# One transposition per block in the later attention chunks: GpSimd adds the two squares of exponentials, VectorE splits them again with triangular masks

## The chip, the cores and the metric

The kernel runs on one core of a Trainium2 chip. The metric is the device time of one execution in microseconds (us). Engines are named as in the profile: PE is TensorE (matrix products), PEld its weight loads, DVE is VectorE, ACT is ScalarE, POOL is GpSimd, SP the engine that issues most DMAs.

## The reference

Attention with 4 sink keys and a window of 128 keys over 4 batches, 8 heads, 768 positions and head size 64, then a two-layer feed-forward on the 3072 tokens that come out (512 to 2048 to 512, with a squared relu between).

```python
scores = (q @ k.T) / sqrt(64)
keep = (key < n_sink) | ((query - key >= 0) & (query - key < window))
a = exp(where(keep, scores, -1e9) - max);  a = a / (sum(a) + 1e-9)
x = (a @ v).transpose(0, 2, 1, 3).reshape(3072, 512)
r = maximum(x @ w_in, 0);  out = (s * r * r + b) @ w_out
```

## The kernel before, in words

**Chunks.** The 3072 tokens are cut into 8 chunks of 384 (half a batch, three blocks of 128 queries). Attention of a chunk gives its x, and the first layer (`l1_steps`, line 680: 16 steps of 12 products `h`) reads x. The attention of the later chunks is woven into the first layer of the chunks ahead of them. Chunks 0 and 2 have code of their own (`first_slots`, `second_slots`); the other six go through `attn_slots`, and only these six are changed. The second layer (`second_layer`, line 805) follows when all chunks are through.

**A unit** is one head and one block of 128 queries; there are 6 x 8 x 3 = 144. Because the window is 128 keys, a block of queries sees two squares of 128 x 128 scores: the *own* square (keys of the same block, where only key <= query is kept) and the square *before* (keys of the block before, where only key > query is kept), and 8 sink columns. The first block of a sequence has no square before; this is so for 16 of the 144 units.

- `unit_a` (slot t): two products into a PSUM bank `sc` (lines 349, 350), DVE adds the mask into SBUF tile `sm` and takes the maximum (354), ACT takes the exponential in place with its sum (360), POOL copies the sink columns into `psk` (362).
- `unit_b` (slot t + 3, `LB`): PE transposes the square before and the own square into a bank `tp` (373, 374), and ACT copies both to the head's tile `tt` (377). After the last block of an odd head come four small DVE operations on the sums and a POOL copy (382 to 387).
- `unit_c` (slot t + 5, `LC`, last block of an odd head): PE multiplies V by the `tt` of both heads into `o` (399), ACT copies `o` to `xm` (403); for every second pair also `ts` and `xsk` (407 to 410).
- `unit_d` (slots t + 7 and t + 8, every second pair): two products `os` and `zb` (421, 423), two DVE operations (424, 425), an ACT cast (426) and a POOL subtraction (427) write x.
- `prep_head`, two slots ahead of a head: ACT and DVE split q and k into parts (330 to 335).

`sm` has SMB = 5 buffers, `tt` has TTB = 4, and PSUM banks rotate among eight.

**Order.** The main loop sorts all pieces by a due position among the first layer's steps and emits them; one attention slot falls to 7 or 8 products `h`, and the steps that prepare the second layer's weights (`early_w2`) are spread in between. A scheduler then fixes the order on each engine; each engine works in that order, and waits where data or a buffer isn't ready. Apart from a few pinned instructions, order is not written by hand.

Of the kernel before, what the change touches and what calls it, by code (L numbers as in the profile page):

```python
# [8 lines left out]
F32 = mybir.dt.float32  # L9
# [5 lines left out]
ALU = mybir.AluOpType  # L15
AX = mybir.AxisListType

P = 128
B, H, S, D = 4, 8, 768, 64
NS = 8  # L20
BLK = 3
CH = BLK * P
# [6 lines left out]
BIG = 3e38  # L29
MDT = mybir.dt.bfloat16  # L30
WUP = 256.0
SMB, TTB = 5, 4
WARM0 = 14
VB = 4
POOLED = 2
# [11 lines left out]
def tile_kernel(ctx, tc, qT, kT, k0, v, vsk, n_sink, window, w1, w2, s, b, out):  # L47
    nc = tc.nc
# [6 lines left out]
    def ps(name):  # L55
        return pools[0].tile([P, 512], F32, tag="a", name=name)
# [5 lines left out]
    wk = wk_cm.__enter__()  # L62
# [18 lines left out]
    ident = identr.bitcast(F32)  # L81
# [5 lines left out]
    msk = wk.tile([P, 3 * W + P + NS], MDT, tag="msk", name="msk", bufs=1)  # L87
    m_1, m_odd, m_even = (msk[:, j * W:(j + 1) * W] for j in range(3))
    m_0 = msk[:, 3 * W:]

# [22 lines left out]
    rel, rel1, low, upp, kix, snk, tmp, tm2 = (sc0[:, j, :] for j in range(8))  # L115


    def mask(out, keep):
        return nc.vector.tensor_scalar(out=out, in0=keep, scalar1=BIG, scalar2=-BIG, op0=ALU.mult, op1=ALU.add)
# [36 lines left out]
    def constants3():  # L156
        pin = tc.keep_in_program_order

        for i, sel in enumerate(sels):
            spread = wk.tile([P, P], F32, tag="y", name="spread", bufs=1)  # L160
            pin(nc.gpsimd.memset(spread, 0.0))
            for j in (i, 2 + i):
                nc.gpsimd.affine_select(
                    out=spread[96:P].rearrange("p (a d) -> p a d", a=2),
                    in_=spread[96:P].rearrange("p (a d) -> p a d", a=2),
                    pattern=[[1, 2], [0, D]], compare_op=ALU.not_equal, fill=1.0, base=2 * j, channel_multiplier=-1)
            nc.scalar.copy(sel, spread)
        for t in psks:
            pin(nc.gpsimd.memset(t, 0.0))
        pin(nc.vector.tensor_tensor(out=tmp[:, :NS], in0=low[:, :NS], in1=snk[:, :NS], op=ALU.mult))  # L170
        nc.vector.tensor_tensor(out=tmp[:, :NS], in0=snk[:, :NS], in1=tmp[:, :NS], op=ALU.subtract)
        pin(nc.vector.scalar_tensor_tensor(out=tm2[:, :NS], in0=rel1[:, :NS], scalar=w_ap, in1=snk[:, :NS],
                                           op0=ALU.is_ge, op1=ALU.mult))
        mask(m_0[:, :NS], tmp[:, :NS])
        mask(m_1[:, 2 * P:], tm2[:, :NS])
        pin(mask(m_even[:, P:P + NS], snk[:, :NS]))
        cp = lambda **a: pin(nc.gpsimd.tensor_copy(**a))
        upm, lom = m_full[2][:, P:2 * P], m_full[2][:, 2 * P:]
        cp(out=m_0[:, NS:], in_=lom)
        for m, l0 in ((m_1, P), (m_even, P + NS), (m_odd, P)):  # L180
            cp(out=m[:, :P], in_=upm)
            cp(out=m[:, l0:l0 + P], in_=lom)
        cp(out=m_odd[:, 2 * P:], in_=m_even[:, P:P + NS])
# [153 lines left out]
    def unit_a(k, h, i):  # L337

        hd = k.heads[h]
        pp = k.pairs[h // 2]  # L340
        g = k.half * BLK + i
        u = (k.c * H + h) * BLK + i
        if k.half == 0:
            c0, n = ((0, P + NS), (NS, W), (P + NS, W))[i]
        else:
            c0, n = ((0, W), (P, W), (W, W))[i]
        sc = ps("sc")
        qs = slice(i * P, (i + 1) * P)
        nc.tensor.matmul(sc[:, :n], hd.qs[:, qs], hd.kh[:, c0:c0 + n], start=True, stop=False)  # L349
        nc.tensor.matmul(sc[:, :n], hd.qs[:, qs], hd.kl[:, c0:c0 + n], start=False, stop=True)  # L350
        m = m_0 if g == 0 else m_1 if g == 1 else m_odd if g % 2 else m_even
        uu = slice(u, u + 1)
        sm = wk.tile([P, W], F32, name="sm", tag="sm", bufs=SMB)
        nc.vector.tensor_tensor_reduce(out=sm[:, :n], in0=sc[:, :n], in1=m, scale=-0.125, scalar=BIG,  # L354
                                       op0=ALU.add, op1=ALU.min, accum_out=negm[:, uu])

        k.cc[(h, i)] = (sm,) + ((NS, None, 0) if g == 0 else (P, 0, 2 * P) if g % 2 else (P + NS, 0, P))
        s0 = k.cc[(h, i)][3]
        hh = h % 2
        nc.scalar.activation(sm[:, :n], sm[:, :n], AF.Exp, bias=negm[:, uu], scale=-1.0, accum_out=pp.zz[:, i, hh:hh + 1])  # L360
        r0 = h % 4 * NS
        nc.gpsimd.tensor_copy(out=pp.psk[:, i, :96].rearrange("p (t x) -> p t x", t=3)[:, :, r0:r0 + NS],  # L362
                              in_=sm[:, s0:s0 + NS].unsqueeze(1).to_broadcast([P, 3, NS]))

    def unit_b(k, h, i):

        sm, c0, p0, _ = k.cc.pop((h, i))
        hd = k.heads[h]
        if i == 0:
            hd.tt = wk.tile([P, 8 * P], F32, name="tt", tag="tt", bufs=TTB)  # L370
        tp = ps("tp")
        if p0 is not None:
            nc.tensor.transpose(tp[:, :P], sm[:, p0:p0 + P], ident)  # L373
        nc.tensor.transpose(tp[:, P:2 * P], sm[:, c0:c0 + P], ident)  # L374

        a, z = (P if p0 is None else 0), 2 * P
        nc.scalar.copy(hd.tt[:, i * z + a:(i + 1) * z], tp[:, a:z])  # L377
        pp = k.pairs[h // 2]
        if h % 2 == 1 and i == BLK - 1:
            zr = wk.tile([P, 2, BLK, 2], F32, tag="zr", name="zr")  # L380
            zh = wk.tile([P, BLK, 2], F32R, tag="zh", name="zh")
            nc.vector.tensor_scalar(out=zr[:, 0], in0=pp.zz, scalar1=1e-9, scalar2=None, op0=ALU.add)
            nc.vector.reciprocal(out=zr[:, 1], in_=zr[:, 0])
            nc.vector.tensor_copy(zh, zr[:, 1])
            r0 = 96 + h // 2 % 2 * 2
            nc.gpsimd.tensor_copy(out=pp.psk[:, :, r0:r0 + 2], in_=zh.bitcast(F32))
            nc.vector.tensor_tensor(out=pp.psk[:, :, r0 + 4:r0 + 6], in0=zr[:, 1], in1=zh.bitcast(F32), op=ALU.subtract)
# [41 lines left out]
    def attn_slots(chunks):  # L429


        units, ahead = [], {}
        for k in chunks:
            for pr in range(H // 2):
                h, t0 = 2 * pr, len(units)
                units += [(k, h + hh, i) for hh in range(2) for i in range(BLK)]
                todo = ((-5, load_pair, pr), (-5, load_keys, h), (-2, load_sinks, pr), (-2, prep_head, h), (-2, load_keys, h + 1),
                        (1, prep_head, h + 1))
                for d, fn, a in todo:
                    ahead.setdefault(max(t0 + d, 0), []).append((fn, k, a))  # L440
        n = len(units)

        def slot(t):
            def f():
                for fn, k, a in ahead.get(t, ()):
                    fn(k, a)
                for fn, lag in ((unit_a, 0), (unit_b, LB), (unit_c, LC),
                                (lambda *u: unit_d(*u, -1), LC + LD), (lambda *u: unit_d(*u, 0), LC + LD + 1)):
                    if 0 <= t - lag < n:
                        fn(*units[t - lag])  # L450
            return f

        return [slot(t) for t in range(n + LC + LD + 1)]
# [571 lines left out]
    k, slots = first_slots()  # L1025
# [16 lines left out]
    t2 = H * BLK * t1 - LEAD  # L1042
    dt = (n_last - LEAD - t2) / len(rows)
    todo = [(max(t * t1 - LEAD, 0.3), f) for t, f in enumerate(plain)] + [(t2 - 2, constants3), (t2, scalars)]
    todo += [(t2 + t * dt, f) for t, f in enumerate(rows)]
    todo += [(NF + (t + 0.5) * (n_last - LEAD - NF) / n_early, lambda: next(early)()) for t in range(n_early)]
# [97 lines left out]
```

## Time and profile before

| | |
|---|---|
| median of 3 runs | 707.59 us (705.12 to 709.23) |
| the profiled execution | 706.58 us |
| its span from the first to the last instruction | 704.7 us |
| PE, PEld | busy 687.7 us (98%), 645.0 us (92%) |
| DVE, ACT | busy 506.0 us (72%), 505.1 us (72%) |
| POOL | busy 102.5 us (15%) |

The profile is of one execution; its time is 1.9 us more than its span. Busy shares are means over stages: start (to about 100 us), first layer with the later attention (100 to about 400 us), rest of the first layer (to about 450 us), second layer. Product records overlap, since products are pipelined, so the duration of one is more than what it adds to PE's time.

### The profile page before, as it was taken

To read this page: it belongs to the slowest core of one execution; us is meant where nothing else is said; L and a number is where in the kernel's file an instruction comes from. 1 tells how busy PE (TensorE), PEld (TensorE's weight loads), DVE (VectorE), ACT (ScalarE), POOL (GpSimd) and SP (SyncE) were. 2 spreads that over 40 slices of the span, in tenths; PEclk is the share of its full clock that TensorE was granted. 3 is DMA by queue.
4 is the path that set the end of the run, shared out by engine and by line. 5 is a ranking of instruction groups with operands and counts; after the bars stand their busy time and mean duration, and the time that the engine had idled before them with its cause. 6 is when DMAs were issued, how large, how long until landed. Compare 5 with 4: busy or idle time off the path is not lost.

```text
span 704.7 us, 13755 instructions
## 1 busy us (share of the span) xinstructions
PE 687.7 (98%) x4858; PEld 645.0 (92%) x4858; DVE 506.0 (72%) x1266; ACT 505.1 (72%) x1155; POOL 102.5 (15%) x249
## 2 busy tenths in 40 slices
PE   8999999999999999999999999999999999999994
PEld 4686789999999999999999999999999999999994
DVE  5999974765864765765766526688979897888883
ACT  3899778788788888888888636576666666657560
POOL 2303011322321331331331210000000000000000
PEclk9999999999999999999999999999999999999998
DMA  8952264466456566454453149933535344443522
GB/s 167 412 199 86 95 193 140 127 214 230 135 189 229 152 226 226 125 178 143 150 181 123 68 180 316 320 97 102 164 104 176 94 150 120 120 150 102 169 60 65
DMA packets 61182, 114.10 MB, mean 162 GB/s; under 512 B 8369, under 2 KB 37169, under 8 KB 58289
## 3 DMA queue, kind: packets, MB, share of 16 engines
q1 hardware_dynamic: 59584, 107.43, 47.6%
q0 software_dynamic: 432, 5.51, 2.3%
q8 instruction: 40, 0.66, 0.4%
q10 hardware_dynamic: 1088, 0.20, 0.2%
q14 instruction: 38, 0.30, 0.1%
HBM read 76.16 MB, written 36.96 MB: 161 GB/s over the span
## 4 chain that ended last, share of the span: by engine, by line
PE 89%; DVE 4%; ACT 2%; DMA 2%; issue 1%; DVEq 0%; ACTq 0%
PE h L680 37%; PE Q L805 32%; PE o L399 5%; PE sc L350 2%; PE sc L349 2%; PE tp L374 2%; PE tp L373 2%; PE sc L492 1%; DMA gs<-gs 1%; PE o L636 1%; PE ts L407 1%; PE wp L98 1%; PE sc L587 1%; DMA kraw<-in_kT 1%; PE os L421 1%
## 5 line engine op out<-in xcount | busy, mean ns | idle before, releaser
L680 PE MATMUL h<-x,w 128*128 128x384 f32 x1536 | 307.6, 344 | 0.0
L680 PEld LDWEIGHTS h<-x,w 128*128 128x128 f32 x1536 | 262.6, 188 | 7.6 <-issue 5.7
L805 PE MATMUL Q<-v,gH 128*128 128x256 f32 x1008 | 128.3, 283 | 0.0
L805 PEld LDWEIGHTS Q<-v,gH 128*128 128x128 f32 x1008 | 124.2, 192 | 0.3 <-issue 0.2
L773 ACT ACTIVATE gs<-gs,sbu 128x1024 f32<-128x1024 f32 x48 | 55.3, 1151 | 71.9 <-DMA gs<-gs 67.7
L354 DVE CUSTOM_DVE_ANT_0 sm<-sc,msk 128x264 f32<-128x264 f32 (+1 forms) x144 | 59.7, 415 | 60.6 <-PE sc L350 55.2
L805 PE MATMUL Q<-v,gA 128*128 128x256 f32 x756 | 99.0, 283 | 1.4 <-DVE gA L784 1.4
L805 PEld LDWEIGHTS Q<-v,gA 128*128 128x128 f32 x756 | 94.4, 192 | 1.7 <-DVE gA L784 1.6
L686 ACT ACTIVATE g<-h 128x384 f32<-128x384 f32 x128 | 61.8, 486 | 29.7 <-PE h L680 21.9
L360 ACT ACTIVATE sm<-sm,negm 128x264 f32<-128x264 f32 (+1 forms) x144 | 72.8, 506 | 10.2 <-DVE negm L354 9.0
L362 POOL COPY psk<-sm 128x24 f32<-128x24 f32 x144 | 32.8, 228 | 209.5 <-ACT sm L360 208.5
L786 DVE TENSOR_TENSOR gH<-gs,gH 128x1024 fp32r<-128x1024 f32 x48 | 58.6, 1220 | 3.5 <-ACT gH L785 3.5
L783 ACT ACTIVATE gA<-gs,sbu 128x512 fp32r<-128x512 f32 x96 | 53.7, 606 | 6.6 <-PE Q L805 6.6
L785 ACT CAST gH<-gs 128x1024 fp32r<-128x1024 f32 x48 | 49.9, 1039 | 11.4 <-DVE gs L778 5.8
L377 ACT COPY tt<-tp 128x256 f32<-128x256 f32 (+1 forms) x144 | 50.8, 354 | 6.2 <-PE tp L374 5.6
L784 DVE SCALAR_TENSOR_TENSOR gA<-gs,sbu,gA 128x512 fp32r<-128x512 f32 x96 | 54.9, 613 | 0.0
L775 DVE SCALAR_TENSOR_TENSOR gs<-gs,sbu 128x256 f32<-128x256 f32 x48 | 23.2, 483 | 37.0 <-ACT gs L773 37.0
L349 PE MATMUL sc<-kh,qs 128*128 128x264 f32 (+1 forms) x144 | 40.1, 279 | 0.8 <-DVE x L640 0.8
L350 PE MATMUL sc<-kl,qs 128*128 128x264 f32 (+1 forms) x144 | 40.9, 284 | 0.0
L374 PE MATMUL tp<-identr,sm 128*128 128x128 f32 x144 | 39.4, 274 | 0.0
L334 DVE TENSOR_TENSOR qs<-qraw,qs 64x384 fp32r<-64x384 f32 x48 | 28.8, 600 | 11.5 <-ACT qs L330 10.1
L333 ACT CAST kh<-kraw 128x528 fp32r<-128x528 f32 (+1 forms) x48 | 28.6, 596 | 11.5 <-PE sc L349 7.2
(177 smaller groups left out, 1015.6 us busy)
## 6 DMA issues: line engine op xcount, KB each, us to landing
gs<-g SPq DMA_DIRECT2D x64, 384.0 KB, 3.1
gs<-gs SPq DMA_DIRECT2D x48, 512.0 KB, 4.2
kraw<-in_kT SPq DMA_DIRECT2D x32, 264.0 KB, 2.8
wraw<-in_w SPq DMA_DIRECT2D x8, 1024.0 KB, 11.0
vraw<-in_w SPq DMA_DIRECT2D x6, 1024.0 KB, 5.7
wd<-v SPq DMA_DIRECT2D x3, 1792.0 KB, 5.8
v<-wd POOLq DMA_DIRECT2D x3, 1792.0 KB, 9.6
out<-ot SPq DMA_DIRECT2D x10, 512.0 KB, 3.2
```

The lines of the kernel that those rows point to most:

```text
L349: nc.tensor.matmul(sc[:, :n], hd.qs[:, qs], hd.kh[:, c0:c0 + n], start=True, stop=False)
L350: nc.tensor.matmul(sc[:, :n], hd.qs[:, qs], hd.kl[:, c0:c0 + n], start=False, stop=True)
L354: nc.vector.tensor_tensor_reduce(out=sm[:, :n], in0=sc[:, :n], in1=m, scale=-0.125, scalar=BIG, op0=ALU.add, op1=ALU.min, accum_out=negm[: ...
L360: nc.scalar.activation(sm[:, :n], sm[:, :n], AF.Exp, bias=negm[:, uu], scale=-1.0, accum_out=pp.zz[:, i, hh:hh + 1])
L374: nc.tensor.transpose(tp[:, P:2 * P], sm[:, c0:c0 + P], ident)
L680: nc.tensor.matmul(h[:, :CH], w_in(f, wi)[:, cc * P:(cc + 1) * P], k.x[xi][:, cc, :], start=(i == 0), stop=(i == len(order) - 1))
L686: nc.scalar.activation(g["r"][:, f % 2], h[:, :CH], AF.Relu, scale=1.0 / WUP)
L773: nc.scalar.activation(g[:, 0], g[:, 0], AF.Square, scale=root_ap)
L783: nc.scalar.activation(o[:, :, 0], x, AF.Identity, bias=b1_ap, scale=1.0)
L784: stt(out=o[:, :, 1], in0=x, scalar=b1_ap, in1=o[:, :, 0].bitcast(F32), op0=ALU.add, op1=ALU.subtract)
L786: nc.vector.tensor_tensor(out=H[:, :, 1], in0=S, in1=H[:, :, 0].bitcast(F32), op=ALU.subtract)
L805: nc.tensor.matmul(bank[:, rb], left[j][:, gi, rb * P:(rb + 1) * P], right[j][:, wi], start=(q == 0 and (rb == 0 or parted) and i == 0), s ...
```

## The change

Before `unit_b`, in `unit_a`, POOL adds the square before onto the own square, in place. The two hold no key in common (each is zero where the other is kept), so the sum loses nothing. `unit_b` does nothing for the first two blocks of a head. For the third it transposes the three summed squares into one bank, and one DVE product with two triangular masks (`tri`, made once) writes both squares of all three blocks to `tt` (768 columns), in place of three ACT copies. `sm` gets a sixth buffer.

```diff
-SMB, TTB = 5, 4
+SMB, TTB = 6, 4
@@ tile_kernel
+    tri = wk.tile([P, 2, P], MDT, tag="tri", name="tri", bufs=1)
@@ constants3
+        for j, op in enumerate((ALU.is_gt, ALU.is_le)):
+            pin(nc.vector.tensor_scalar(out=tri[:, j], in0=rel, scalar1=0.0, scalar2=None, op0=op))
@@ unit_a, behind the exponential
+        c0, p0 = k.cc[(h, i)][1:3]
+        if p0 is not None:
+            own, before = sm[:, c0:c0 + P], sm[:, p0:p0 + P]
+            nc.gpsimd.tensor_tensor(out=own, in0=own, in1=before, op=ALU.add)
@@ unit_b
-        sm, c0, p0, _ = k.cc.pop((h, i))
+        if i < BLK - 1:
+            return
         hd = k.heads[h]
-        if i == 0:
-            hd.tt = wk.tile([P, 8 * P], F32, name="tt", tag="tt", bufs=TTB)
         tp = ps("tp")
-        if p0 is not None:
-            nc.tensor.transpose(tp[:, :P], sm[:, p0:p0 + P], ident)
-        nc.tensor.transpose(tp[:, P:2 * P], sm[:, c0:c0 + P], ident)
-
-        a, z = (P if p0 is None else 0), 2 * P
-        nc.scalar.copy(hd.tt[:, i * z + a:(i + 1) * z], tp[:, a:z])
+        for j in range(BLK):
+            sm, c0 = k.cc.pop((h, j))[:2]
+            nc.tensor.transpose(tp[:, j * P:(j + 1) * P], sm[:, c0:c0 + P], ident)
+        hd.tt = wk.tile([P, 8 * P], F32, name="tt", tag="tt", bufs=TTB)
+        shape = [P, BLK, 2, P]
+        nc.vector.tensor_tensor(
+            out=hd.tt[:, :2 * CH].rearrange("p (i t c) -> p i t c", i=BLK, t=2),
+            in0=tp[:, :CH].rearrange("p (i c) -> p i c", i=BLK).unsqueeze(2).to_broadcast(shape),
+            in1=tri.unsqueeze(1).to_broadcast(shape), op=ALU.mult)
         pp = k.pairs[h // 2]
-        if h % 2 == 1 and i == BLK - 1:
+        if h % 2 == 1:
```

What stands on PE in the second half of a pair, from the transpositions of an odd head's last block to just before V's product with its `tt`. Before (line numbers of the kernel before; `h` are first-layer products; the rows that follow are `tp` twice and then `o`):

```order
L373 MATMUL tp<-identr,sm 128x128
L374 MATMUL tp<-identr,sm 128x128
L680 MATMUL h<-x_3_2399,w_1010 128x384 x6
L349 MATMUL sc<-kh,qs 128x264
L350 MATMUL sc<-kl,qs 128x264
L373 MATMUL tp<-identr,sm 128x128
L374 MATMUL tp<-identr,sm 128x128
L680 MATMUL h<-x_3_2399,w_1010 128x384 x2
L680 MATMUL h<-x_3_2400,w_1010 128x384 x4
L680 MATMUL h<-x_4_3148,w_443 128x384 x3
L349 MATMUL sc<-kh,qs 128x264
L350 MATMUL sc<-kl,qs 128x264
```

The same place now (`h` is line 689, `sc` 352 and 353, `tp` 380, `o` 408):

```order
L380 MATMUL tp<-identr,sm 128x128 x3
L689 MATMUL h<-x_3_2349,w_1013 128x384 x6
L352 MATMUL sc<-kh,qs 128x264
L353 MATMUL sc<-kl,qs 128x264
L689 MATMUL h<-x_3_2349,w_1013 128x384 x2
L689 MATMUL h<-x_3_2350,w_1013 128x384 x4
L689 MATMUL h<-x_4_3065,w_444 128x384 x3
L352 MATMUL sc<-kh,qs 128x264
L353 MATMUL sc<-kl,qs 128x264
L408 MATMUL o<-tt,v_p 64x256 x2
```

The transpositions of three blocks stand together, and 15 products `h` and two pairs of `sc` lie between them and `o`, as before.

DVE around the two slots in which `unit_d` writes x, before (`vt`, `vraw` belong to the second layer's weights; the second `L354` row of each pair reads the maximum):

```order
L424 TENSOR_TENSOR xm<-os,xm 128x384
L382 TENSOR_SCALAR zr<-zz 128x6
L425 TENSOR_TENSOR xm<-zb,xm 128x384
L243 ISA vraw_1985<-vraw_1985,vt 128x1024x2
L354 ISA sm,negm<-sc,msk 128x264
L354 ISA negm 128x1
L424 TENSOR_TENSOR xm<-os,xm 128x384
L383 RECIPROCAL zr<-zr 128x6
L425 TENSOR_TENSOR xm<-zb,xm 128x384
L384 CAST zh<-zr 128x6
L387 TENSOR_TENSOR psk_103<-zr,zh 128x3x2
L354 ISA sm,negm<-sc,msk 128x264
```

And now (424, 425 are 433, 434; 354 is 357; the masked product is 383):

```order
L433 TENSOR_TENSOR xm<-os,xm 128x384
L337 TENSOR_TENSOR qs<-qraw,qs 64x384
L434 TENSOR_TENSOR xm<-zb,xm 128x384
L246 ISA vraw_1952<-vraw_1952,vt 128x1024x2
L338 TENSOR_TENSOR kl<-kraw,kh 128x528
L357 ISA sm,negm<-sc,msk 128x264
L357 ISA negm 128x1
L433 TENSOR_TENSOR xm<-os,xm 128x384
L357 ISA sm,negm<-sc,msk 128x264
L357 ISA negm 128x1
L434 TENSOR_TENSOR xm<-zb,xm 128x384
L383 TENSOR_TENSOR tt<-tp,tri 128x768
```

The masked product stands right behind both `unit_d` groups, so it takes whatever lateness they have.

POOL in the same kind of place before (`x` is written by `unit_d`, `vs` by the sinks' load):

```order
L322 TENSOR_TENSOR vs<-vsraw,vs 32x128
L362 COPY psk_103<-sm 128x3x8
L427 TENSOR_TENSOR x_3_2400<-xm,x_3_2399 128x384
L322 TENSOR_TENSOR vs<-vsraw,vs 32x128
L362 COPY psk_103<-sm 128x3x8
L386 COPY psk_103<-zh 128x3x2
```

And now (427 is 436, 362 is 369, 322 is 325; the sum of the squares is 367):

```order
L325 TENSOR_TENSOR vs<-vsraw,vs 32x128
L367 TENSOR_TENSOR sm<-sm 128x128
L369 COPY psk_104<-sm 128x3x8
L325 TENSOR_TENSOR vs<-vsraw,vs 32x128
L436 TENSOR_TENSOR x_1_1625<-xm,x_1_1624 128x384
L367 TENSOR_TENSOR sm<-sm 128x128
L369 COPY psk_104<-sm 128x3x8
```

Every sink copy now has a sum ahead of it, and both may stand behind the subtraction that writes x.

## Rows read from the trace of the kernel before

**Rows 1.** Busy time by stretch: PE, PEld, DVE, ACT, POOL, clock, DMA share, GB/s.

```profile
100.00:400.00 300.00, 300.00 (x2044) 283.95 (x2043) 191.09 (x574) 249.45 (x703) 79.36 (x207) 1.00 0.52 168
204.00:210.00 6.00, 6.00 (x41) 6.00 (x39) 5.42 (x17) 5.16 (x16) 2.84 (x6) 1.00 0.63 209
```

**Rows 2.** Waits of PE from 90 to 465 us: all that the view lists.

```profile
PE Q L805 <- DVE gA L784: 1.4, 1, 1.4
PE sc L349 <- DVE x L640: 0.8, 1, 0.8
```

**Rows 3.** Chain that ended last, 100 to 400 us: shares by line.

```profile
by line: PE h L680 64.7%; PE o L399 10.5%; PE sc L350 5.6%; PE sc L349 5.2%; PE tp L374 5.2%; PE tp L373 4.5%; PE ts L407 1.8%; PE os L421 1.3%; PE zb L423 1.3%
```

**Rows 4.** The chain around a pair's end: start us, us, what.

```profile
203.56 0.12 PE sc L349
203.69 0.12 PE sc L350
...
209.72 0.12 PE sc L349
209.84 0.12 PE sc L350
209.97 0.11 PE tp L373
210.08 0.11 PE tp L374
210.19 1.58 PE h L680 x9
211.77 0.06 PE sc L349
211.83 0.11 PE sc L350
```

**Rows 5.** Groups by line, 100 to 400 us: busy us, mean ns, idle before.

```profile
L374 PE MATMUL tp<-identr,sm 128*128 128x128 f32 x139 | 38.1, 274 | 0.0
L373 PE MATMUL tp<-identr,sm 128*128 128x128 f32 x123 | 33.4, 272 | 0.0
```

**Rows 6.** Groups by line, whole span: copies, weight loads, DVE operations that read PSUM.

```profile
L377 ACT COPY tt<-tp 128x256 f32<-128x256 f32 (+1 forms) x144 | 50.8, 354 | 6.2 <-PE tp L374 5.6
...
L373 PEld LDWEIGHTS tp<-identr,sm 128*128 128x128 f32 x128 | 17.9, 140 | 0.0
...
L424 DVE TENSOR_TENSOR xm<-os,xm 128x384 f32<-128x384 f32 x24 | 13.1, 548 | 1.8 <-PE os L421 1.8
...
L818 DVE TENSOR_TENSOR u<-Q,u 128x512 f32<-128x512 f32 x18 | 12.4, 687 | 0.3
```

**Rows 7.** Operations with two SBUF inputs, 100 to 400 us: duration ns min/median/max.

```profile
L322 POOL TENSOR_TENSOR vs<-vsraw,vs x22: 452/457/1504, 128.0 to 390.3; 32x128 fp32r<-32x128 f32 x22
L427 POOL TENSOR_TENSOR x<-xm,x x22: 1007/1033/1452, 129.7 to 391.5; 128x384 fp32r<-128x384 f32 x22
L334 DVE TENSOR_TENSOR qs<-qraw,qs x45: 551/554/1136, 100.3 to 385.4; 64x384 fp32r<-64x384 f32 x45
```

**Rows 8.** The same lines' means, 100 to 400 us.

```profile
L322 POOL TENSOR_TENSOR vs<-vsraw,vs 32x128 fp32r<-32x128 f32 x22 | 15.9, 722 | 7.1 <-POOL psk L362 2.4 <-POOL x L427 2.0 <-POOL psk L386 1.9
L334 DVE TENSOR_TENSOR qs<-qraw,qs 64x384 fp32r<-64x384 f32 x45 | 27.1, 603 | 11.4 <-ACT qs L330 10.1
```

**Rows 9.** DVE in order of time around the pair's end of rows 4.

```profile
208.72 0.56 DVE L425 TENSOR_TENSOR xm<-zb,xm 128x384 f32<-128x384 f32 x1
209.33 1.23 DVE L706 TENSOR_TENSOR v<-vT,v 128x1024 fp32r<-128x1024 f32 x1
210.47 0.43 DVE L354 CUSTOM_DVE_ANT_0 sm<-sc,msk 128x264 f32<-128x264 f32 x1
210.82 0.08 DVE L354 DVE_READ_ACCUMULATOR2_ANT negm<- 128x1 f32 x1
211.76 0.77 DVE L334 TENSOR_TENSOR qs<-qraw,qs 64x384 fp32r<-64x384 f32 x1 [0.85 <-ACT qs L330]
...
213.18 0.29 DVE L354 CUSTOM_DVE_ANT_0 sm<-sc,msk 128x136 f32<-128x136 f32 x1
```

**Rows 10.** The exponential and the `o` product that belong to rows 4.

```profile
204.42 0.52 ACT L360 ACTIVATE sm<-sm,negm 128x264 f32<-128x264 f32 x1
204.84 0.19 ACT L360 ACTIVATION_READ_ACCUMULATOR sm<-sm,negm 128x1 f32 x1
...
213.52 1.30 PE L399 MATMUL o<-tt,v_p 128*64 128x256 f32 x12
```

**Rows 11.** The boundary to the second layer in the chain.

```profile
436.57 11.19 PE h L680 x64
447.76 0.76 ACT g L686 x2
448.52 0.04 issue
448.56 1.14 DVE gA L784 x2
449.70 1.15 DVE gH L786
450.85 0.02 issue
450.86 7.33 DMA gs<-gs
```

## The prediction

> **What bounds the kernel now.** I read four views, in this order. First the busy times by stretch. The change touches only the attention of the six later chunks, which lies between about 100 and 400 us, so it is that stretch's row that counts and not the page's mean: there PE is busy for all 300 us, ACT for 249, DVE for 191 (64%), POOL for 79 (26%) [rows 1]. Second, PE's waits, since a busy share alone doesn't tell that PE is the bound (records of products overlap): from 90 to 465 us PE waits 2.2 us in all, at two places, and neither is a transposition or an `o` product [rows 2]. Third, the chain that ended last: from 100 to 400 us it consists of PE lines alone, whose shares add up to 100% [rows 3]. So whatever takes time from PE here shortens the span, as long as the other engines still deliver in time. Fourth, the order of time around one pair's end, for how much time they have [rows 4, 9, 10].
>
> **What it takes from PE.** 144 units had 128 transpositions on line 373 and 144 on line 374; now there are 144. So 128 go. The groups give 272 ns for one [rows 5], but that is the length of a pipelined record and not what it adds: of 300 us the chain gives line 373 4.5%, or 13.5 us, over 123 records [rows 3, 5], which is 0.110 us each; single pieces read 0.11 [rows 4]. 128 x 0.110 = **14.1 us**. Bounds: 13.4 us if a piece is 0.105 us rounded up; 17.9 us if the weight load of a transposition sets the pace (140 ns each, 17.9 us in all) [rows 6]. I take the chain's price, since the chain is what adds up to the span.
>
> **What it takes from ACT.** 144 copies, 50.8 us, all but a few of them in the stretch [rows 6]. ACT comes to about 200 of 286 us, 70%. It isn't the bound, so I count nothing for that.
>
> **What it adds on DVE.** 48 products of 768 columns that read PSUM. None is in the trace. Nearest are 384 columns in 548 ns and 512 in 687 [rows 6], so 139 ns per 128 columns and 687 + 2 x 139 = 965 ns. Bounds: 687 (not cheaper than 512 columns) and 2 x 548 = 1096. In all 46.3 us, so DVE comes to 237 of 286 us, 83%. What hides it is DVE's idle time, 109 us in the stretch now [rows 1]. The two mask operations in `constants3` are 128 columns each, under 548 ns each; the start has room for them, and 1 us is their most.
>
> **What it adds on POOL.** 128 sums of 128 columns with two SBUF inputs. Nearest is line 322, also 128 columns: 457 ns median, 722 on average; line 427 (384 columns, 1007 ns at least) gives a lower bound of a third, 336 [rows 7, 8]. I take 457 ns: 58 us, so POOL has 138 of 286 us, 48%; with 722 it is 60%. POOL isn't full either way.
>
> **Do the new waits reach PE?** Three have to be looked at.
> (1) Transposition behind POOL's sum. For the unit whose scores start at 203.56, the exponential is through at 205.03 [rows 4, 10], and its transposition, three slots later, starts at 209.97: 4.9 us. The sum takes 0.46, at worst 1.5 [rows 7], and ahead of it in POOL's order can stand a subtraction (1.0 to 1.5) and a sinks' operation. About 1 to 3 us are left. The first two blocks of a head wait longer than before, so more is left.
> (2) `o` behind the masked product. Transpositions end at 210.19 and `o` starts at 213.52 [rows 4, 10], 3.3 us; the two transpositions that stood between, 0.22 us, go, and the product takes 0.97: DVE may start it **2.1 us** late. The same is true of every pair, as the order shows 15 `h` and two pairs of `sc` in between. How late is DVE? At this pair, which lies in a `unit_d` stretch, it is at its fullest: 5.42 of 6.00 us [rows 1]. The `sc` that ended at 209.97 was taken up at 210.47, 0.5 us late; the one that ended at 211.94 at 213.18, 1.2 us late [rows 4, 9]. The masked product would stand behind the operation of 210.47 and run from about 210.9 to 211.9, much of it in the 0.85 us in which DVE waited for ACT's `qs`; `o` needs it at about 213.3. In such a stretch 6.4 us of work meet 5.7 us of PE time, so lateness grows by 0.7 us, to 1.9 us where it was 1.2. That just fits. There are 12 such stretches; I put **1 us** on the total for those that don't fit.
> (3) Buffers. The first block's `sm` is now held until slot t + 5. The sixth buffer's next writer comes in slot t + 6, and its `sc` products stand behind those transpositions on PE, so it can't wait for them. PSUM: one `tp` bank per head in place of three, so the eight banks turn more slowly.
> Behind the masked product on DVE stands the next unit's mask operation, whose `sm` has the slack of (1); later than before by up to 1 us, it still has it.
>
> **The sum.** Span 704.7 - 14.1 + 1.0 = 691.6; with 1.9 outside the span 693.5. The profiled execution was 1.0 below the median of the runs shown, so the median comes to **694.5 us**, 1.8% less. At the boundary to the second layer, the chain leads from the last `h` through ACT and DVE to a 7.33 us transfer [rows 11]: it starts when the first layer ends, and moves forward with it.
>
> **A rule that speaks against it.** POOL and DVE hinder each other where both read two SBUF inputs: line 322 takes 457 ns mostly and up to 1504, line 334 on DVE 554 and up to 1136 [rows 7]. The Trainium skill, "GPSIMD Engine Reference", Specifications, says that GpSimd's SBUF interfaces are shared with VectorE, with contention against DVE instructions that have two SBUF inputs; its section on engine selection sends elementwise sums to VectorE. By that the third rival would be likelier than I make it; by the means of the rows DVE lost only 49 ns per `qs` operation (603 against 554) [rows 7, 8], 2.2 us over the stretch, while POOL lost 265 ns per line 322. So POOL gives way, mostly, and has room. I count nothing in the sum.
>
> **The rivals.**
> *VectorE late* (0.20): the 0.7 us of each of the 12 stretches is paid in full, 8.4 us, since lateness adds up to more than 2.1 us. About 702 (698 to 706). For it: 90% busy in those stretches. Against: the other heads have slack (between 100 and 400 us a third of DVE's time is idle).
> *The gain isn't there* (0.07): the removed transpositions ran in time that something else needed anyway. About 707. Against it: no waits on PE, and a DMA share of 0.52 [rows 1].
> *The shared port* (0.08, slower): every sum keeps DVE out for its length. DVE then has 237 us plus 128 times that length; from 0.49 us per sum, this is over 300 us and DVE sets a later end than before. With the 722 ns mean it is 330 us, some 30 us more than the stretch takes now: about 737. With 457 ns it would still be 703. For it: the maxima above. Against: sums fall on `sm`, and most of DVE's time goes to operations with one operand in PSUM, which lost nothing (548 ns mean at 384 columns).
> *My forecast* (0.65): 691 to 698. Its low end has the weight loads' 17.9 us.
>
> **Range and chances.** 690 to 703 holds the forecast and most of the first rival, some 0.8. A measurement of this kernel can tell about 0.5%, 3.5 us, from no change: faster means below 704.0. Forecast and four fifths of the first rival: 0.80. Within 0.5%: 0.09. Slower, the third rival and some of the second: 0.11.
>
> **What would show it.** Right: PE lines alone in the chain between 100 and 390 us; 144 transpositions; no PE or PEld wait for `tt` or `sm` beyond 1 us in all; masked product near 965 ns; sum near 460 to 720 ns; DVE near 83% and ACT near 70% of the stretch. Wrong: PE waiting at `o` for DVE (first rival) or at `tp` for POOL (a sum much longer than 0.72 us); `qs` and `kl` operations on DVE much longer than 603 ns (third); transpositions in groups of three that take more than 0.11 us each.

## The result, and the profile after

| | before | after |
|---|---|---|
| median | 706.36 us (4 runs, 704.51 to 709.23) | 694.09 us (4 runs, 692.98 to 695.25) |
| ratio | | 0.983, 95% interval 0.980 to 0.985 |
| the profiled execution, its span | 706.58, 704.7 us | 695.25, 693.5 us |

The changed kernel is 12.3 us faster; 694.5 was forecast. Of all executions in this document one, of the kernel with the sum on DVE, took 1672.6 us in place of some 701 and is left out of its median. Again I read first the busy times of the stretch, here from 100 to 386 us (columns as in [rows 1]):

```profile
100.00:386.00 286.00, 284.58 (x1898) 268.69 (x1897) 232.90 (x607) 208.19 (x559) 140.10 (x326) 1.00 0.54 175
```

DVE is busy for 81% (83% was worked out), ACT for 73% (70%), POOL for 49% (48%). PE, which was busy for all of it, now lacks 1.4 us. The groups by line, 100 to 390 us, that answer to [rows 5 to 8] (busy us, mean ns, idle before):

```profile
L367 POOL TENSOR_TENSOR sm<-sm 128x128 f32<-128x128 f32 x123 | 63.1, 513 | 122.9 <-ACT sm L363 111.8 <-PE tp L380 5.1 <-PE sc L353 1.6
...
L383 DVE TENSOR_TENSOR tt<-tp,tri 128x768 f32<-128x768 f32 x47 | 44.7, 951 | 0.0
...
L369 POOL COPY psk<-sm 128x24 f32<-128x24 f32 x139 | 42.8, 308 | 8.4 <-ACT sm L363 8.3
...
L338 DVE TENSOR_TENSOR kl<-kraw,kh 128x528 fp32r<-128x528 f32 (+1 forms) x45 | 32.7, 727 | 9.4 <-ACT kh L336 9.0
L337 DVE TENSOR_TENSOR qs<-qraw,qs 64x384 fp32r<-64x384 f32 x45 | 30.7, 683 | 3.7 <-ACT qs L333 2.0
...
L380 PE MATMUL tp<-identr,sm 128*128 128x128 f32 x138 | 22.5, 272 | 0.0
```

The masked product takes 951 ns (965 was worked out from 384 and 512 columns), the sum 513. One price was not in the sum: `qs` on DVE, 603 ns in [rows 8], takes 683 now. Line 338 of the kernel after splits the keys; it takes 727 (677 before the change).

PE's waits from 90 to 455 us, which answer to [rows 2]:

```profile
PE Q L814 <- DVE gA L793: 1.5, 1, 1.5
PE o L408 <- DVE tt L383: 0.9, 1, 0.9
PE sc L352 <- ACT g L695: 0.6, 1, 0.6
PE sc L353 <- DVE kl L338: 0.5, 1, 0.5
```

Two are new: `o` waited for the masked product, and `sc` for the keys. The list shows less than there is. A wait of some tenths of a microsecond within a group of products is covered by the record of the product before it. So I compared the `o` groups in order of time. Ahead of the change those of 16 records take 1.52 us and those of 12 take 1.30, without exception. After it, six of 24 between 100 and 400 us take longer, 2.8 us in all. The two largest, with what stands around them:

```profile
183.31 0.28 PE L353 MATMUL sc<-kl,qs 128*128 128x264 f32 x1
183.52 1.87 PE L408 MATMUL o<-tt,v_p 128*64 128x256 f32 x16
...
257.75 0.28 PE L353 MATMUL sc<-kl,qs 128*128 128x264 f32 x1
257.97 0.65 PE L408 MATMUL o<-tt,v_p 128*64 128x256 f32 x2
259.56 1.51 PE L408 MATMUL o<-tt,v_p 128*64 128x256 f32 x14 [0.95 <-DVE tt L383]
```

The first has 1.87 in place of 1.52. In the second the first two records, of the even head, go, and the rest, which begins with the odd head, stands until 259.56: 1.6 us more than a whole group. All six are pairs whose masked product stands behind the two `unit_d` groups. DVE ahead of the second:

```profile
252.20 0.18 DVE L392 RECIPROCAL zr<-zr 128x6 f32<-128x6 f32 x1
254.73 0.71 DVE L338 TENSOR_TENSOR kl<-kraw,kh 128x528 fp32r<-128x528 f32 x1 [2.35 <-ACT kh L336]
255.36 0.42 DVE L357 CUSTOM_DVE_ANT_0 sm<-sc,msk 128x264 f32<-128x264 f32 x1
...
257.07 1.21 DVE L715 TENSOR_TENSOR v<-vT,v 128x1024 fp32r<-128x1024 f32 x1
258.21 0.42 DVE L357 CUSTOM_DVE_ANT_0 sm<-sc,msk 128x264 f32<-128x264 f32 x1
258.56 0.07 DVE L357 DVE_READ_ACCUMULATOR2_ANT negm<- 128x1 f32 x1
258.56 0.94 DVE L383 TENSOR_TENSOR tt<-tp,tri 128x768 f32<-128x768 f32 x1
```

DVE isn't too busy here: it stands idle for 2.35 us at the keys, with everything queued behind them. The chain that ended last says what the keys waited for (start us, us, what):

```profile
245.16 0.16 issue
245.32 0.09 DVE negm L357
245.43 0.61 ACT sm L363 x2
246.04 0.39 ACT g L695
246.44 0.53 SPq L697
246.97 0.05 issue
247.01 0.03 SPq L315
247.04 0.03 issue
247.07 6.97 DMA kraw<-in_kT
254.07 0.64 ACT kh L336
254.73 0.03 DVE kl L338
```

Before the change this chain consisted of PE lines alone [rows 3]. Now it leaves PE for a late load of keys, which took 6.97 us (3.0 is the median in its line). `kraw` has one buffer, so a load can't start before DVE has split the keys that lie there. The same place before the change, and then now:

```profile
249.73 0.71 DVE L335 TENSOR_TENSOR kl<-kraw,kh 128x528 fp32r<-128x528 f32 x1
251.07 1.30 PE L399 MATMUL o<-tt,v_p 128*64 128x256 f32 x12
...
245.03 1.30 PE L408 MATMUL o<-tt,v_p 128*64 128x256 f32 x12
245.32 0.69 DVE L338 TENSOR_TENSOR kl<-kraw,kh 128x528 fp32r<-128x528 f32 x1
```

The split before ended 0.6 us ahead of the start of the `o` group, and now it ends 1.0 us behind it, so the buffer comes free 1.6 us later. The rest isn't the buffer's: the transfer took 6.97 us where it took 5.46 before, and no run shows why. (In both kernels SP issued the load 1.1 us after the split, behind a store of `gs`.)

### The profile page after: what moved, and what is told of

It is laid out like the page before. It is cut to its first block, busy times and chain, and to the rows that moved or that the text cites. A ratio compares the mean times of both kernels' runs of the same rounds, so it can differ in the third digit from the quotient of the medians.

```text
span 693.5 us, 13721 instructions
## 1 busy us (share of the span) xinstructions
PE 675.9 (97%) x4730; PEld 633.2 (91%) x4730; DVE 551.8 (80%) x1316; ACT 464.4 (67%) x1011; POOL 168.5 (24%) x377
## 4 chain that ended last, share of the span: by engine, by line
PE 67%; DVE 12%; DMA 11%; ACT 4%; issue 3%; SPq 1%; POOL 0%; ACTq 0%; DVEq 0%
PE h L689 34%; PE Q L814 16%; DMA gs<-gs 8%; PE o L408 4%; DVE gA L793 2%; PE sc L353 2%; PE sc L352 2%; PE tp L380 2%; ACT gs L782 2%; DMA kraw<-in_kT 2%; DVE gH L795 1%; PE o L541 1%; DVE u L827 1%; PE o L645 1%; DMA q<-in_qT 1%
## 5 line engine op out<-in xcount | busy, mean ns | idle before, releaser
L689 PE MATMUL h<-x,w 128*128 128x384 f32 x1536 | 303.1, 342 | 0.0
L367 POOL TENSOR_TENSOR sm<-sm 128x128 f32<-128x128 f32 x128 | 65.4, 511 | 133.1 <-ACT sm L363 122.0
L357 DVE CUSTOM_DVE_ANT_0 sm<-sc,msk 128x264 f32<-128x264 f32 (+1 forms) x144 | 58.9, 411 | 17.2 <-PE tp L380 12.1
L369 POOL COPY psk<-sm 128x24 f32<-128x24 f32 x144 | 44.3, 308 | 8.4 <-ACT sm L363 8.3
L383 DVE TENSOR_TENSOR tt<-tp,tri 128x768 f32<-128x768 f32 x48 | 45.7, 951 | 0.7 <-PE tp L380 0.7
L338 DVE TENSOR_TENSOR kl<-kraw,kh 128x528 fp32r<-128x528 f32 (+1 forms) x48 | 34.9, 728 | 9.5 <-ACT kh L336 9.0
L408 PE MATMUL o<-tt,v_p 128*64 128x256 f32 (+1 forms) x352 | 36.6, 338 | 0.9 <-DVE tt L383 0.9
## 6 DMA issues: line engine op xcount, KB each, us to landing
wraw<-in_w SPq DMA_DIRECT2D x8, 1024.0 KB, 10.6
```

The source lines that it names most:

```text
L367: nc.gpsimd.tensor_tensor(out=own, in0=own, in1=before, op=ALU.add)
L408: tc.keep_in_program_order(nc.tensor.matmul(o[hh * D:(hh + 1) * D, q0:q0 + n * P], pp.v[:, kb, hh, :], k.heads[h - 1 + hh].tt[:, c0 * P:(c ...
L689: nc.tensor.matmul(h[:, :CH], w_in(f, wi)[:, cc * P:(cc + 1) * P], k.x[xi][:, cc, :], start=(i == 0), stop=(i == len(order) - 1))
```

## The experiments

Each kernel ran beside the kernel before. "Stretch" is a measure of my own, from the first start of an `sc` product to the last in the profiled execution; it leaves out the start and the second layer, which the change doesn't touch and which differ by some microseconds between executions of the same code. Times in us; ratio to the kernel before on the same chip. The kernel before itself had medians from 704.58 to 706.36 us on these chips, so a difference of 1 or 2 us between two rows is read from ratio and stretch and not from the medians alone.

| kernel | median | ratio, 95% interval | stretch | `o` groups over length |
|---|---|---|---|---|
| before | 706.36 | 1 | 307.2 | none |
| changed | 694.09 | 0.983 (0.980 to 0.985) | 296.4 | 6 of 24 |
| changed, again | 694.32 | 0.984 (0.982 to 0.987) | 295.9 | 6 |
| only the transpositions removed | 693.34 | 0.984 (0.980 to 0.988) | 294.3 | none |
| masked product twice | 704.64 | 0.999 (0.997 to 1.002) | 305.6 | 15 of 23 |
| sum twice | 694.92 | 0.985 (0.981 to 0.989) | 298.0 | 5 |
| sum on DVE | 701.24 | 0.994 (0.992 to 0.997) | 303.7 | 8 of 23 |
| no sum | 691.62 | 0.979 (0.977 to 0.981) | 294.3 | 3 |
| unit_c a slot later | 694.19 | 0.986 (0.983 to 0.988) | 294.0 | none |
| five `sm` | 693.52 | 0.985 (0.982 to 0.988) | 294.9 | 2 |
| two `kraw` | 689.58 | 0.978 (0.976 to 0.979) | 293.6 | 2 |
| two `kraw`, again | 690.26 | 0.980 (0.977 to 0.982) | 293.7 | 1 |
| before with two `kraw` | 702.76 | 0.997 (0.995 to 0.999) | 307.0 | none |
| before with six `sm` | 704.24 | 0.999 (0.996 to 1.002) | 306.6 | none |

**PE alone.** From the kernel before, only what the change takes from PE.

```diff
         tp = ps("tp")
-        if p0 is not None:
-            nc.tensor.transpose(tp[:, :P], sm[:, p0:p0 + P], ident)
         nc.tensor.transpose(tp[:, P:2 * P], sm[:, c0:c0 + P], ident)
...
-        nc.scalar.copy(hd.tt[:, i * z + a:(i + 1) * z], tp[:, a:z])
+        nc.scalar.copy(hd.tt[:, i * z + a:(i + 1) * z].rearrange("p (t c) -> p t c", c=P),
+                       tp[:, P:2 * P].unsqueeze(1).to_broadcast([P, (z - a) // P, P]))
```

> The kernel before, with only the 128 transpositions of the square before left out; ACT's copy takes the own square twice, so it is as long as it was, and DVE and POOL are as before (part of the attention's arithmetic is left out). My theory, that PE alone bounds the stretch and a transposition is worth its 0.110 us in the chain: 14.1 us less than the kernel before, about 692.5 us. Rival, that the gain of the change came from ACT having less to do: no change, about 706. If the whole weight load of 0.140 us counts: 17.9 us less, about 688.5.

Its median is 12.0 us below the kernel before on the same chip (705.38), and the stretch 13.0 us shorter. ACT is as busy as before, and PE is busy for all of it (100 to 386 us, columns as in [rows 1]; the kernel before, then this one):

```profile
100.00:386.00 286.00, 286.00 (x1950) 270.68 (x1949) 181.66 (x542) 240.02 (x674) 73.63 (x194) 1.00 0.54 173
100.00:386.00 286.00, 286.00 (x1917) 269.90 (x1916) 190.96 (x571) 244.72 (x701) 81.73 (x207) 1.00 0.54 175
```

So the gain is PE's, and it comes without ACT's lighter load. The stretch holds 124 of the 128 transpositions that go, so one was worth 13.0 / 124 = 0.105 us. PE has one wait in this stretch, at its start, which the change doesn't touch and which [rows 2] has with 0.8 us:

```profile
PE sc L349 <- DVE x L639: 1.4, 1, 1.4
```

Without the 0.6 us that it is longer here, a transposition comes to 13.6 / 124 = 0.110 us. Either way it isn't the 0.140 of its weight load.

**The masked product twice.** What is DVE's time worth?

```diff
-        nc.vector.tensor_tensor(
+        for _ in range(2):
+            nc.vector.tensor_tensor(
...
```

> The changed kernel, with the masked product on DVE made twice in a row, so DVE has 48 x 0.95 = 46 us more, 279 of 286 us. My theory, that a pair's o product has about 2 us of slack and the stretches in which x is written are already at that limit: the second product is paid in part, about 10 us, some 704 us. Rival, that DVE's time is already paid in full: 46 us more, about 740. Rival, that DVE is hidden anyway: no change, 694.

704.64: 46 us more on DVE cost 10.3 to 10.6 us, and 9.2 to 9.7 us in the stretch. DVE's time is neither free nor paid in full at this load; about a fifth comes through to PE. The second product also makes each `tt` 0.95 us later, and this run doesn't tell that from the fuller DVE; the sums on DVE, below, stand elsewhere in its order and cost about the same share.

**The sum twice.**

```diff
+            twin = wk.tile([P, P], F32, tag="twin", name="twin", bufs=1)
+            nc.gpsimd.tensor_tensor(out=twin, in0=own, in1=before, op=ALU.add)
             nc.gpsimd.tensor_tensor(out=own, in0=own, in1=before, op=ALU.add)
```

> The changed kernel, with every sum on POOL made once more into a tile of its own, so POOL has 128 x 0.51 = 65 us more, 205 of 286 us. My theory, that POOL has room and gives way where both engines read two SBUF inputs: within 1.5 us of the changed kernel, 694 to 695.5. Rival, the shared port (each sum keeps DVE out): DVE operations with two SBUF inputs get longer again, as they did with the change (qs from 603 to 683 ns, kl from 677 to 727), DVE gets later, and the time rises by 4 us or more, 698 and above.

694.92, within the bound: 0.6 to 0.8 us above the changed kernel, with POOL busy for 197 of 286 us. The keys on DVE grow to 764 ns, but `qs` falls to 649, and the 4 us or more of the shared-port rival don't come. A second sum isn't free, though. The stretch is 1.6 to 2.1 us longer, and PE waited for POOL itself, at a transposition behind a second sum:

```profile
PE tp L382 <- POOL sm L369: 1.2, 1, 1.2
```

**The sum on DVE.**

```diff
-            nc.gpsimd.tensor_tensor(out=own, in0=own, in1=before, op=ALU.add)
+            nc.vector.tensor_tensor(out=own, in0=own, in1=before, op=ALU.add)
```

> The changed kernel, with the sums on DVE in place of POOL. A sum of 128 columns on DVE is taken as 0.29 us (400 columns take 565 ns, 139 ns less per 128 columns), 37 us in all, so DVE has 270 of 286 us. My theory: POOL as the place is right, DVE gets late by some 5 us in all, about 699. Rival (the rule that sums belong on VectorE, since GpSimd is slower at them and shares its port): equal to the changed kernel or faster, 694 or less.

701.24, 6.9 to 7.2 us slower than the changed kernel: the direction that I gave, and somewhat more than the 5. A sum on DVE takes 301 ns, all 128 of them 38.5 us, so again about a fifth is paid:

```profile
L367 DVE TENSOR_TENSOR sm<-sm 128x128 f32<-128x128 f32 x120 | 35.9, 301 | 18.8 <-ACT sm L363 17.9
```

The rule of the Trainium skill, "GPSIMD Engine Reference", engine selection, that elementwise sums belong on VectorE, holds for one operation by itself (301 ns against 513) and not for this kernel, in which DVE is busy for 81% of the stretch and POOL for 49%.

**No sum.**

```diff
-            own, before = sm[:, c0:c0 + P], sm[:, p0:p0 + P]
-            nc.gpsimd.tensor_tensor(out=own, in0=own, in1=before, op=ALU.add)
+            pass
```

> The changed kernel without POOL's sums (the square before is left out of the attention). Theory, that the sums are hidden and cost DVE some 7 us in collisions: qs back from 683 to about 603 ns, kl from 727 to about 677, and the time within 1.5 us of the changed kernel, 692.5 to 694. Rival, the shared port as what limits: 690 or less.

691.62, some 2.6 us below the changed kernel and 0.9 below the range given. `qs` is back at 597 ns and the keys at 694:

```profile
L338 DVE TENSOR_TENSOR kl<-kraw,kh 128x528 fp32r<-128x528 f32 (+1 forms) x45 | 31.2, 694 | 7.6 <-ACT kh L336 7.2
L337 DVE TENSOR_TENSOR qs<-qraw,qs 64x384 fp32r<-64x384 f32 x45 | 26.8, 597 | 1.6
```

So the collisions are real: 45 operations at 86 and 45 at 33 ns are 5.4 us of DVE's time. I had counted nothing for them. The stretch is 1.6 to 2.1 us shorter. How much of that the collisions made and how much the sums themselves, by coming late, isn't shown, since this run takes away both; at the fifth found above, 5.4 us of DVE's time would be 1.1 us (an estimate).

**unit_c one slot later.**

```diff
-LB, LC, LD, L2, LEAD, PIECES = 3, 5, 2, 2, 2, 4
+LB, LC, LD, L2, LEAD, PIECES = 3, 6, 2, 2, 2, 4
```

> The changed kernel with unit_c one slot later (LC = 6), so the masked product may start about 4 us late in place of 2, and unit_d one slot later too. Theory, that what the change loses is PE waiting within o for the odd head's tt: all o groups are 1.52 or 1.30 us, and the time falls by some 2.5 us, about 691.5. Rival, that PE's own work is all there is: no change, 694. Rival, that x gets late for the next chunk's first products: longer, 696 or more.

No `o` group is too long any more, and yet the time is the same, 694.19. The stretch is shorter only because six products `h` and one `o` group now stand behind its end; from the last `sc` to the second layer it takes 56.4 us in place of 53.8, and the two together are 350.4 us, where the changed kernel has 350.2 and 349.7. PE's waits from 90 to 400 us:

```profile
PE h L689 <- POOL x L436: 1.0, 2, 0.6
PE sc L352 <- ACT g L695: 0.6, 1, 0.6
PE os L430 <- DVE xsk L419: 0.3, 1, 0.3
```

Part of the wait, 1.0 us of it in this list, has moved to the first products that need the new x. My theory that slack at `o` gives the loss back was wrong: `o` is where the lateness came out, not what made it.

**Two kraw buffers.**

```diff
-            hd.k = wk.tile([P, KW], F32, tag="kraw", name="kraw", bufs=1)
+            hd.k = wk.tile([P, KW], F32, tag="kraw", name="kraw", bufs=2)
```

> The changed kernel with two buffers for the keys as loaded (kraw) in place of one. Theory: part of the lateness is a chain, in which a late DVE frees kraw late, the load starts late beside a 1 MB load, and DVE then stands idle at kl with the masked product queued behind; with two buffers the 1.6 us at one pair go, and the time falls by 1 to 2 us, about 692.5. Rival, that DVE's own work makes all the lateness: no change, 694, and the o groups get as long as before.

> The changed kernel with two buffers for kraw once more, since its first trace explains 2 of its 4.7 us only (stretch with scores 293.6 us against 295.9, o groups 34.9 against 36.6): 690 to 692 if the rest was the scatter of executions in the parts that the change doesn't touch, 689.5 again if it belongs to the buffer.

> The kernel before with two buffers for kraw in place of one, and nothing of the change. Theory, that the second buffer only takes away what the change made late: no change from the kernel before, within 2 us, since PE waits for nothing there. Rival, that the buffer is worth its 4.7 us by itself (690 against 694): some 4 us less than the kernel before, about 701.

The changed kernel with it takes 689.58 and 690.26 us, by the ratios 2.1 to 4.7 us less than without, and is the fastest version here. The load of the same keys now starts 12.1 us ahead of their split (at 237.06) in place of 7.7 (at 247.07); DVE has no wait there, and `o` has its usual length:

```profile
249.16 0.71 DVE L338 TENSOR_TENSOR kl<-kraw,kh 128x528 fp32r<-128x528 f32 x1
249.79 0.54 DVE L434 TENSOR_TENSOR xm<-zb,xm 128x384 f32<-128x384 f32 x1
...
254.59 0.94 DVE L383 TENSOR_TENSOR tt<-tp,tri 128x768 f32<-128x768 f32 x1
```

```profile
255.61 1.52 PE L408 MATMUL o<-tt,v_p 128*64 128x256 f32 x16
```

The chain that ended last, from 100 to 390 us, consists of PE lines alone again:

```profile
by line: PE h L689 68.2%; PE o L408 11.0%; PE sc L353 5.7%; PE sc L352 5.4%; PE tp L380 5.3%; PE ts L416 1.8%; PE os L430 1.4%; PE zb L432 1.3%
```

The stretch is 2.3 to 2.8 us shorter in both of its traces, and ACT's 7.2 us of waits for `kraw` are gone. In the kernel before the second buffer leaves the stretch as it was (307.0). So the single buffer mattered only once DVE ran later. What stays open is the rest: the medians say some 4 us, and the kernel before with two buffers has 1.8 us less too, with the same stretch. That rest lies in parts that the change doesn't touch (in the traces, the start and the second layer). Whether the buffer moves something there or executions scatter, no run tells apart; from the second layer's first product to the end the traces have 250.8 to 256.5 us, and the lowest is of a kernel with one buffer.

**The sixth `sm` buffer**, taken from the change and given to the kernel before.

```diff
-SMB, TTB = 6, 4
+SMB, TTB = 5, 4
```

> The changed kernel with five sm buffers in place of six. Each third unit's mask operation on DVE then waits for the three transpositions of the same slot, 0.33 us behind its scores, so DVE gets 48 x 0.33 = 16 us of idle time. Theory: 1 to 3 us more than the changed kernel, 695 to 697. Rival, that the sixth buffer isn't needed: 694. Rival, that it makes the change work: 700 or more.

> The kernel before with six sm buffers, the one part of the change that stands by itself. Theory: no change, within 2 us of the kernel before, since PE waits for nothing. Rival, that part of the gain is the buffer's: 2 us or more less.

693.52 and 704.24: no difference either way. My price of 1 to 3 us for its absence was wrong: DVE's idle time ahead of its mask operations (100 to 390 us) rose by 2.5 us, from 16.1 to 18.6, and not by 16, and the stretch isn't longer.

## Why the prediction was right

- *The bound*: right. PE alone set the stretch's length, and what was taken from PE came out as time, with ACT, DVE and POOL as they were.
- *The price of a transposition*: right. 0.110 us from the chain's shares; 0.105 to 0.110 measured without the 128. The 272 ns of the record would have given 35 us, the weight load 17.9.
- *The added operations*: the masked product 951 ns for 965, the sum 513 for 457 with a mean bound of 722.
- *The new waits*: the place was right (the pairs behind `unit_d`, 6 of the 12), the size was not. From the first `sc` product to the second layer, which takes in all 128 transpositions, the kernel before takes 361.3 us and the changed one 350.2 and 349.7, so 11.1 and 11.6 us less; the transpositions are worth 13.4 to 14.1. The term "1 us for those that don't fit" was thus 1.8 to 3.0 us. Two things were missing from it. I looked for work that makes DVE late, and not for what a late DVE then frees late, `kraw`, whose load must follow. And I counted nothing for the collisions of POOL's sums with DVE's splits, 5.4 us of DVE's time.
- *The signs that it named*: mixed. The masked product, the sum and the shares of DVE and ACT came out as said. But the chain left PE, `o` waited for DVE (0.9 us on PE, 1.6 on its weight loads), which was to speak for the first rival, and `qs` took 683 ns, a weak form of the sign of the third. With two `kraw` buffers the first two signs are right again.
- *Why it landed on 694.5 all the same*: luck in part. The forecast took 13.1 us from 707.59, the median of three executions of the kernel before; with the fourth that median is 706.36, 1.2 us lower. Of the 13.1 us, the first four runs show 12.3 and the later ones 11.2, since the loss was taken too low. The two errors are of like size and cancel, and the executions scatter by as much.
- *The rivals*: VectorE late is what part of the gain went to, at a fifth to a third of the price given. The shared port was real in the records; in the time, all that the sums cost was some 2 us of the stretch. That the gain isn't there is refuted.

## What to carry to other kernels

Where one engine is busy all the time and waits for nothing, an instruction is worth its pace in the chain and not the length of its record, and work may go to engines with time to spare even if each operation is slower there. Add to it the price of lateness: ask not only whether the new work fits but which single buffer the engine frees, because behind a load that starts late the engine can stand idle for longer (2.35 us at one pair here) than the new operation takes (0.95 us). A wait that disappears without a gain has moved; measure the whole stretch, not the place.

## What the runs showed that I had not expected

POOL's sum takes 513 ns of its own and makes DVE's operations with two SBUF inputs longer (`qs` 603 to 683, 597 again without the sums). The copy behind it on POOL takes 308 ns where it was 229 before the change; without the sums it takes 259, but with the sums on DVE 308 too, so what makes it longer stays open. A sum made twice doesn't double that: `qs` is at 649. At 81% load 46 us more on DVE cost 10 us and 38 us cost 7, so a fifth of them.
